# Forgetting attention and a bilinear feed-forward on one core: another source for the idle matmuls, masks on GpSimd for one more batch, merged reciprocals, and a new order on all engines

## The chip, the cores and the metric

The kernel runs on one core of a Trainium2 chip. The core has five engines that run their own instruction streams and wait for each other through semaphores: TensorE (PE, matrix products; its weight loads are shown as PEld), VectorE (DVE), ScalarE (ACT), GpSimd (POOL) and SyncE (SP, which here only issues transfers). Sixteen DMA engines move data between device memory and the on-chip buffer (SBUF), or within it; products land in PSUM. The metric is the time of one execution on the device in microseconds (us).

## What is computed

The attention scores of 8 batches with 8 heads, 576 positions and head size 64 get a decay from cumulated logarithms, a causal mask and a softmax; the result goes through a feed-forward part without a nonlinearity but for a product.

```python
scores = scale * np.matmul(q, k.transpose(0, 1, 3, 2))
log_f = np.log(np.clip(f, 0.0001, 1.0))
cum = np.cumsum(log_f, axis=-1)
decay = cum[:, :, :, None] - cum[:, :, None, :]
scores = np.where(causal, -1000000000.0, scores + decay)
attn = softmax(scores)            # along the last axis
x = np.matmul(attn, v)            # heads side by side: 4608 x 512
out = ((x @ w_a) * (x @ w_b)) @ w_out   # 512 -> 1536 -> 512
```

Inputs and outputs are float32; products take float16.

## The kernel before

A unit of attention is a head pair t = 4 b + pr: two heads of batch b, of 32 such pairs. The 576 queries are five blocks i = 0 to 4 (four of 128, one of 64). For each, PE forms the scores in PSUM (tile `sc`), DVE adds the decay and takes the row maximum (`do_decay`, L673, into `S`; in batch 0 the decay is added by PE and DVE only takes the maximum, `do_max`, L645), ACT takes the exponential and the row sums (`do_exp`, L704, into `PA` for blocks 0 to 2 and `PB` for blocks 3 and 4), DVE takes the reciprocal of the sums (`do_recip`, L712 and L714), POOL or ACT scales the rows with it (`do_norm`, L725 and L723), the scaled block is transposed (by PE into `psP` in batch 0 and for blocks 0 to 2 of batch 1, by DMA into `PTA` and `PTB` otherwise), and PE multiplies it with the values (`pv`, `pvx`). The rows of the decay for all keys stand in `spread`, three buffers that are used in turn; for batch 1 PE and an eviction fill them, later a DMA from `cum_d`.

The causal mask is made in two ways. For head pairs outside `MASKP` PE adds a product of two constants, `neg` and `low`, to the diagonal blocks of `sc`. For those in it, POOL writes masked copies of the diagonal blocks of `spread` (`mask_copy`, L630, and `mask_last`, L637), so that the decay carries the mask; PE then computes blocks 1 and 2 in two pieces, the diagonal block first. `PSPREAD` are the four pairs of batch 1, `EARLY` batches 0 and 1.

The feed-forward part runs over pieces of 256 to 512 tokens: PE forms `psa` and `psb` (L74), ACT copies `psa` to `a`, DVE multiplies (`ht`, L1072), PE forms `pso` and ACT or DVE evicts it (`osb`) for the store. The last 1024 tokens are done by a scheme with fewer products (tiles `wg`, `wb`, `og`, `om`), which fills the last 60 us. The feed-forward pieces of earlier batches fill PE between the attention steps of later ones.

At the start PE has nothing to do until q and k have landed. `wake` gives it idle matmuls, 24 times four, which read the identity matrix; their sums are never used. POOL issues the loads of the weights: each of w_a and w_b in four pieces, columns 0 to 511 and columns 512 to 1535, each for both halves of the partitions.

What sets the order: the kernel writes every step as an `Op` in a list and then runs through a table `ORDER` of their numbers. Each engine executes its own steps in that order, so a step that waits holds everything behind it on its engine. `CHOICE` says for each step that several engines could do which of them does it, and `SLOTS` which buffer of a ring each tile takes. SP's queue holds, in the order of that table as well, the loads of q, k and v, of `spread`, the transposing DMAs and the stores; POOL's queue holds the loads of the weights and of the first batches among its own work.

## Time and profile before

| | us |
|---|---|
| three runs | 392.8, 396.06, 396.86 |
| median | 396.06 |
| span of the profiled execution | 394.4 |
| busy in it: PE, DVE, ACT, POOL | 381.1, 329.1, 299.4, 281.0 |
| granted TensorE clock, mean | 0.999 |

The profiled execution's own time is given as its span, from the first to the last instruction; the time of a run has what lies around it as well. Busy times are unions of an engine's instructions. A matmul's end is modelled, and matmuls overlap, so the start of the next one tells what one costs. In the page's slices each digit is the busy share of a fortieth of the span in tenths:

```profile
DVE  7888898998996888788788888757898899987992
ACT  4998999999886878868888588779899672556331
POOL 8689686768867689874899769578976891267600
PEclk9999999999999999999999999999999999999999
```

The clock is granted in full throughout. DVE, ACT and POOL are all loaded in the first quarter, and POOL does nothing in the last slices.

### The profile page before, as it was taken

The numbers are of one execution on the slowest core, as the hardware profiler recorded it, in microseconds if no ns is written. First come the engines' busy times: TensorE is split into PE (matmuls) and PEld (weight loads), VectorE is DVE, ScalarE is ACT, GpSimd is POOL, SyncE is SP. The second block draws the span as 40 slices with busy tenths as digits, with TensorE's granted clock in tenths as the row PEclk, the third lists the DMA queues.
The fourth block names the chain that finished last, engine by engine and source line by source line (L and its number), as shares of the span: only waits on it lengthen the run. The fifth ranks groups of instructions, "written<-read, shape, count | busy, mean of one in ns | idle before, by whom it ended". The sixth has DMA issues, their size and how long they took to land.

```text
span 394.4 us, 14909 instructions
## 1 busy us (share of the span) xinstructions
PE 381.1 (97%) x5816; PEld 253.9 (64%) x5816; DVE 329.1 (83%) x1035; ACT 299.4 (76%) x826; POOL 281.0 (71%) x482
## 2 busy tenths in 40 slices
PE   7899999999998999999899999999999999999996
PEld 3557887968765665655555655555555667666796
DVE  7888898998996888788788888757898899987992
ACT  4998999999886878868888588779899672556331
POOL 8689686768867689874899769578976891267600
PEclk9999999999999999999999999999999999999999
DMA  7999999999999999999998999999998898100005
GB/s 121 251 202 170 144 154 223 228 278 275 208 222 215 220 282 247 281 187 277 260 237 255 262 207 229 206 244 263 226 226 195 169 182 178 55 1 2 2 2 214
DMA packets 147190, 76.88 MB, mean 195 GB/s; under 512 B 124336, under 2 KB 128176, under 8 KB 147120
## 3 DMA queue, kind: packets, MB, share of 16 engines
q1 hardware_dynamic: 132824, 68.79, 77.9%
q0 software_dynamic: 14256, 7.08, 14.7%
q8 instruction: 45, 0.74, 0.8%
q14 instruction: 25, 0.20, 0.2%
q10 hardware_dynamic: 40, 0.07, 0.1%
HBM read 52.05 MB, written 9.58 MB: 156 GB/s over the span
## 4 chain that ended last, share of the span: by engine, by line
PE 73%; DMA 11%; DVE 5%; POOL 4%; ACT 3%; issue 2%; ACTq 0%; DVEq 0%; POOLq 0%
PE psa L74 15%; PE psb L74 15%; PE pso L74 13%; PE wg L74 5%; DMA PTA<-PA 5%; PE wb L74 4%; PE sc L550 3%; PE og L74 3%; DMA PTB<-PB 3%; PE pvx L768 3%; PE psT L358 2%; DVE S L673 2%; DMA wb<-in_moe_w_b_dram 2%; POOL PA L725 2%; PE wake L74 2%
## 5 line engine op out<-in xcount | busy, mean ns | idle before, releaser
L673 DVE CUSTOM_DVE_ANT_0 S<-sc,spread 64x576 f32<-64x576 f32 (+4 forms) x232 | 125.5, 561 | 14.5 <-ACT PA L704 4.8
L725 POOL TENSOR_SCALAR PA<-PA,st 128x256 f16<-128x256 f16 (+2 forms) x180 | 85.0, 481 | 9.6 <-DVE st L714 6.0
L74 PE MATMUL psb<-xT,wb 128*64 128x512 f16 (+2 forms) x864 | 88.7, 332 | 0.4 <-DVE ht L1072 0.2
L704 ACT ACTIVATE PA<-S,st 128x256 f16<-128x256 f32 (+2 forms) x168 | 84.1, 503 | 6.4 <-DVE st L673 5.8
L74 PE MATMUL psa<-xT,wa 128*64 128x512 f16 (+2 forms) x864 | 88.9, 333 | 0.0
L74 PE MATMUL pso<-wout,ht 128*64 128x512 f16 x672 | 81.8, 381 | 0.0
L725 POOL TENSOR_SCALAR PB<-PB,st 128x512 f16<-128x512 f16 (+1 forms) x90 | 63.6, 713 | 25.3 <-DVE st L714 8.8
L74 PEld LDWEIGHTS <-wb 128*64 128x64 f16 x960 | 55.9, 110 | 24.9 <-issue 1.8
L74 PEld LDWEIGHTS <-wa 128*64 128x64 f16 x960 | 55.2, 110 | 24.7 <-issue 2.2
L1072 DVE TENSOR_TENSOR ht<-psb,a 128x512 f16<-128x512 f32 (+1 forms) x90 | 57.5, 648 | 7.2 <-PE psb L74 5.1
L288 ACT CAST a<-psa 128x512 f16<-128x512 f32 (+1 forms) x90 | 49.4, 550 | 18.0 <-PE psa L74 15.8
L74 PEld LDWEIGHTS <-ht 128*64 128x64 f16 x696 | 38.3, 110 | 26.8 <-issue 2.2
L704 ACT ACTIVATE PB<-S,st 128x512 f16<-128x512 f32 x56 | 40.2, 720 | 3.2 <-DVE st L673 2.7
L704 ACT ACTIVATION_READ_ACCUMULATOR PA<-S,st 128x1 f32 x168 | 32.1, 191 | 0.0
L630 POOL TENSOR_SCALAR_AFFINE_SELECT spread<-spread 128x768 f32<-128x768 f32 x24 | 20.8, 866 | 14.0 <-DMA spread<-cum_d 13.9
L700 ACT ACTIVATE PB<-S,st 128x576 f16<-128x576 f32 x28 | 21.7, 776 | 10.7 <-DMA PTB<-PB 4.1
L768 PEld LDWEIGHTS <-nv 128*64 128x64 f16 x640 | 21.8, 110 | 8.5 <-DMA PTA<-PA 2.3
L673 DVE CUSTOM_DVE_ANT_1 S<-sc,spread 128x256 f32<-128x256 f32 x48 | 19.7, 419 | 7.5 <-ACT PB L704 1.6
L1273 POOL TENSOR_TENSOR hy<-wu 128x512 f16<-128x512 f32 x9 | 11.6, 1302 | 19.7 <-DVE wu L1273 19.6
L714 DVE RECIPROCAL st<-st 128x2 f32<-128x2 f32 x128 | 18.1, 156 | 7.2 <-ACT PA L704 3.6
L673 DVE DVE_READ_ACCUMULATOR2_ANT st<- 128x1 f32 (+1 forms) x280 | 22.8, 81 | 0.0
L550 PE MATMUL sc<-kT,qT 64*128 64x512 f16 (+4 forms) x144 | 21.0, 326 | 1.2 <-ACT kT L288 0.4
(156 smaller groups left out, 692.8 us busy)
## 6 DMA issues: line engine op xcount, KB each, us to landing
spread<-cum_d SPq DMA_DIRECT2D x24, 576.0 KB, 6.4
q<-in_q_dram SPq DMA_DIRECT2D x14, 576.0 KB, 5.3
k<-in_k_dram SPq DMA_DIRECT2D x14, 576.0 KB, 5.4
out_dram<-osb SPq DMA_DIRECT2D x29, 256.0 KB, 4.0
v<-in_v_dram SPq DMA_DIRECT2D x24, 256.0 KB, 5.8
wout<-in_moe_w_out_dram POOLq DMA_DIRECT2D x3, 512.0 KB, 8.0
nv<-in_v_dram POOLq DMA_DIRECT2D x8, 128.0 KB, 5.1
wa<-in_moe_w_a_dram POOLq DMA_DIRECT2D x2, 512.0 KB, 7.5
```

The costliest lines, as they stand in the source:

```text
L74: nc.tensor.matmul(out=out[r], lhsT=lhsT[:, r], rhs=rhs, **kw)
L288: nc.scalar.copy(out=out_, in_=in_)
L550: nc.tensor.matmul(out=dst, lhsT=lhsT, rhs=rhs, start=start, stop=stop, skip_group_check=True)
L630: nc.gpsimd.affine_select(out=c[:, :, 0:SM].rearrange("p h (j k) -> p h j k", k=128), in_=c[:, :, SM:2 * SM].rearrange("p h (j k) -> p h j ...
L673: nc.vector.tensor_tensor_reduce(out=o, in0=x, in1=y, scale=-1.0, scalar=3e38, op0=ADD, op1=MIN, accum_out=m)
L700: nc.scalar.activation(out=p_blocks(t, 4), in_=T[("s" if direct else "z", t, 4)], func=EXP, bias=st[:, 8:9], scale=sign, accum_out=st[:, 1 ...
L704: nc.scalar.activation(out=p_blocks(t, i)[:, :, h, :], in_=(T[("s", t, i)][:, h, :] if direct else T[("z", t, i)][:, h * n:h * n + n]).rea ...
L714: nc.vector.reciprocal(out=st[:, 20 + 2 * i:22 + 2 * i], in_=st[:, 10 + 2 * i:12 + 2 * i])
L725: VEC[e].tensor_scalar(out=p, in0=p, scalar1=st[:, c:c + 1], scalar2=1.0, op0=MUL, op1=MUL)
L768: nc.tensor.matmul(out=o[HP[h], 128 * i:128 * i + 128], lhsT=vt[:, j, pr + NP * h, :], rhs=pt[:, base_blk[i] + 2 * block_at(t, i, j) + h, ...
L1072: nc.vector.tensor_tensor(out=ht[:, 0:n_], in0=T.pop(("psb", t0, fbs))[:, 0:n_], in1=T.pop(("a16", t0, fbs))[:, 0:n_], op=MUL)
L1273: VEC[e].tensor_tensor(out=out_, in0=x, in1=y, op=op)
```

## The change

Five things are changed.

1. The idle matmuls read a new tile `spark` (both as weights and as moving operand), which DVE sets to one in a step of its own.
2. `MASKP` takes in the four head pairs of batch 1. POOL writes masked copies for them; the last block of these pairs still gets its mask from PE.
3. Reciprocals are merged. For batches from 2 on one takes blocks 0 to 2 and one blocks 3 and 4; for batches 0 and 1 one takes blocks 0 and 1, one block 2, one blocks 3 and 4. A merged reciprocal needs all exponentials of its blocks, and every scaling of these blocks needs it.
4. Weight loads are issued in another order among POOL's steps.
5. `ORDER`, `CHOICE` and `SLOTS` are new tables. The number of steps falls from 2480 to 2401.

```diff
+    spark = perm.tile([128, 2], FP16, tag="spark", name="spark")
...
-            mm_halves(x, ident16, ident16[:, 0:1].to_broadcast([128, 512]), start=True, stop=True, skip_group_check=True)
+            mm_halves(x, spark[:, 0:1].to_broadcast([128, 128]), spark[:, 0:1].to_broadcast([128, 512]), start=True, stop=True, skip_group_check=True)
...
+    o_s = Op("DVE", 0.1, lambda _: nc.vector.memset(spark, 1.0), prio=-302, name="spark")
...
-        o = Op("PE", 0.427, lambda _: wake(2), [o_i], prio=-290, mode="full", name=f"wake{n}")
+        o = Op("PE", 0.427, lambda _: wake(2), [o_s], prio=-290, mode="full", name=f"wake{n}")
...
-    MASKP = {t for t in range(8, NP * B)}
+    MASKP = {t for t in range(4, NP * B)}
...
-        if g == 3 and t in MASKP:
+        if g == 3 and t in MASKP and t not in PSPREAD:
...
-    def do_recip(t, i):
+    RGROUPS = {True: [(0, 1, 2), (3, 4)], False: [(0, 1), (2,), (3, 4)]}
+
+    def do_recip(t, blocks):
         st = T[("st", t)]
-        if i == 4:
-            nc.vector.reciprocal(out=st[:, 28:29], in_=st[:, 18:19])
-        else:
-            nc.vector.reciprocal(out=st[:, 20 + 2 * i:22 + 2 * i], in_=st[:, 10 + 2 * i:12 + 2 * i])
+        c0, c1 = 2 * blocks[0], 9 if blocks[-1] == 4 else 2 * blocks[-1] + 2
+        nc.vector.reciprocal(out=st[:, 20 + c0:20 + c1], in_=st[:, 10 + c0:10 + c1])
...
-                rc = Op("DVE", 0.16, lambda _, i=i: do_recip(t, i), es, prio=prio(g))
-                st_users.extend(es + [rc])
...
+                for blocks in RGROUPS[b not in EARLY]:
+                    if i not in blocks or not all(x in ex_of for x in blocks):
+                        continue
+                    rc = Op("DVE", 0.16, lambda _, blocks=blocks: do_recip(t, blocks), sum((ex_of[x] for x in blocks), []),
+                            prio=prio(g), name=f"rc{t}.{blocks[0]}")
...
     ORDER = """
-        0 1 29 30 46 2 52 62 5 3 31 37 32 38 33-36 39 40 42 41 53 47 58 4 43 267 262 279 6-9 54 48 10 56 50 44
...
     CHOICE = """
-        DDDDADADADAAPPAPPPAPPAADAPPPPPPAPADDDDPPPAPPPPPDDDDPAAPAPPPADDDADAADAAAADDPPPAPAPPPADDAAPPAPPAPAADADAAA
...
+        DDPPAAADDDADPPPPPPPPPDDADAPPPPPAAPDDADAPPAPPPPPDDDAAAPAAPPPPADADDADDDDAADAPPAPPPPPPADDDPAPPPAPPPDAAAPA
```

What the tables do is seen on three engines. First ACT at the start of the program, before the change: after the two logarithms (`cum_l`) stand two evictions of the transposed q and k (`qT`, `kT`), the load of the table for the exponential, two more evictions, and the first exponentials (`PA`).

```order
L259 ACTIVATE cum_l<-cum_f 96x256
L259 ACTIVATE cum_l<-cum_f 96x320
L286 ACTIVATE qT<-psT 128x576
L288 COPY kT<-psT 128x576
L220 ACT_TABLE_LOAD
L220 ACTIVATE warm<-warm 128x1
L286 ACTIVATE qT<-psT 128x576 x2
L704 ACTIVATE PA,st<-sc_301,st 128x2x128
```

The same place on ACT after the change:

```order
L261 ACTIVATE cum_l<-cum_f 96x256
L261 ACTIVATE cum_l<-cum_f 96x320
L221 ACT_TABLE_LOAD
L221 ACTIVATE warm<-warm 128x1
L288 ACTIVATE qT<-psT 128x576
L290 COPY kT<-psT 128x576 x2
L706 ACTIVATE PA,st<-sc_257,st 128x2x128
```

The table load stands ahead of the first evictions now, and one eviction of k takes the place of two of q. On PE the transposes of the second half of q (from tile `wout`) stood ahead of the first scores and now stand behind them; and ahead of the very first transpose stand nine groups of four idle matmuls where five stood.

Second POOL, from the last setting of constants (`nv`) on, before the change; `PA<-PA` are scalings, `nv<-in_v_dram` loads of v, `wa` and `wb` loads of the weights, `q<-q` and `k<-k` conversions of the next batch:

```order
L113 MEMSET nv_80 64x512
L725 TENSOR_SCALAR PA<-PA,st 128x128
L620 MEMSET spread_84 128x2x64
L304 DMA nv_79<-in_v_dram 128x8x64 x2
L290 TENSOR_SCALAR q_470<-q_184 128x2x9x64
L725 TENSOR_SCALAR PA<-PA,st 128x2x128
L292 CAST k_473<-k_186 128x2x9x64
L725 TENSOR_SCALAR PA<-PA,st 128x2x128
L725 TENSOR_SCALAR PA<-PA,st 128x3x128
L509 DMA wa_76<-in_moe_w_a_dram 64x4x512
```

And after it:

```order
L114 MEMSET nv_81 64x512
L622 MEMSET spread_85 128x2x64
L511 DMA wa_77<-in_moe_w_a_dram 64x4x1024
L306 DMA nv_80<-in_v_dram 128x8x64 x2
L511 DMA wa_77<-in_moe_w_a_dram 64x4x512
L292 TENSOR_SCALAR q_520<-q_295 128x2x9x64
L511 DMA wb_78<-in_moe_w_b_dram 64x4x512
L727 TENSOR_SCALAR PA<-PA,st 128x2x128
L294 CAST k_535<-k_468 128x2x9x64
```

Three loads of weights stand ahead of the first scaling now, the first of them for columns 512 to 1535. The second piece of wa for columns 0 to 511 stood behind six scalings and stands behind thirteen; the last load of wb stood behind 21 scalings and four conversions and stands behind 17 and two. Two subtractions for the low parts of `crow`, which DVE did, stand on POOL ahead of the constants.

Third DVE in the middle of the program, before the change; `ISA S,st` are score additions with their maximum, `ISA st` reads of that maximum:

```order
L1072 TENSOR_TENSOR ht<-psb,a_4120 128x512
L673 ISA S,st<-sc_4047,spread_86 128x384
L673 ISA st 128x1
L1072 TENSOR_TENSOR ht<-psb,a_4173 128x512
L714 RECIPROCAL st<-st 128x2
L673 ISA S,st<-sc_4137,spread_86 64x576
L673 ISA st 64x1
L714 RECIPROCAL st<-st 128x2
L1072 TENSOR_TENSOR ht<-psb,a_4183 128x512
L712 RECIPROCAL st<-st 128x1
```

And after it:

```order
L675 ISA S,st<-sc_3979,spread_85 128x384
L675 ISA st 128x1
L1081 TENSOR_TENSOR ht<-psb,a_3972 128x512
L716 RECIPROCAL st<-st 128x6
L1081 TENSOR_TENSOR ht<-psb,a_4072 128x512
L716 RECIPROCAL st<-st 128x6
L675 ISA S,st<-sc_3974,spread_86 128x512
```

One reciprocal of six columns (blocks 0 to 2, two heads) takes the place of three of two columns, and one of three columns that of one of two and one of one.

On PE, in batch 1, the 64 products of `neg` and `low` for blocks 0 to 3 are gone, and 16 pieces of scores more are formed. Between the first scores of the last head pair and its output products stand 24 groups psa or psb and 10 groups pso (24 and 7 before); behind its scores of block 3 there stand 7 groups psa or psb and 8 pso (12 and 7 before).

More of the change, by code (lines that the diff above doesn't have):

```diff
@@ L154 @@
+        a0123456b78cd0192345678ab0123456789cd0;n16:01010100100100110110100010111101;n32:0120221021212012012002
+        102110202201201020120102012012012010012;nv:0101010101;osb:010111010010010101001010101101;qd:0101010101
+        00101010100101;sc:010101010101010101010101100101011001100001010101001010100110100101010101010100101010
+        1010100101010101010010001010010010100101010001010010101001010;st:01234501234501234501234051203401
     """
```

122 lines of the change are left out of this document (82 added, 40 removed), and 135 rows, old and new, of the table ORDER.

## The prediction

> **What bounds the kernel now.** I read the page first: its span, the busy shares and the slices of PE.
>
> ```profile
> span 394.4 us, 14909 instructions
> PE 381.1 (97%) x5816; PEld 253.9 (64%) x5816; DVE 329.1 (83%) x1035; ACT 299.4 (76%) x826; POOL 281.0 (71%) x482
> PE   7899999999998999999899999999999999999996
> ```
>
> TensorE (PE) is busy 97% of 394.4 us, so at most 394.4 - 381.1 = 13.3 us of open idle time are to be had. But "busy" includes the idle matmuls (tile wake), so I read the first 50 us by windows next. Columns: window, length, then busy us and instructions of PE, PEld, DVE, ACT, POOL.
>
> ```profile
> 10.00:20.00 10.00, 8.84 (x192) 5.28 (x186) 8.65 (x16) 9.70 (x38) 6.59 (x12) 1.00 1.14 253
> 20.00:30.00 10.00, 9.37 (x162) 5.82 (x160) 8.58 (x23) 9.23 (x30) 8.91 (x18) 1.00 1.00 199
> 30.00:40.00 10.00, 9.78 (x198) 7.38 (x196) 8.62 (x17) 8.99 (x22) 9.18 (x15) 1.00 1.08 172
> 40.00:50.00 10.00, 9.79 (x242) 8.67 (x238) 8.09 (x27) 9.23 (x26) 6.19 (x9) 1.00 1.21 134
> ```
>
> From 10 to 40 us ScalarE (ACT) has 27.9 of 30 us, VectorE (DVE) 25.9 and GpSimd (POOL) 24.7, the last of them 6.6 in the first ten and 9.2 in the last ten. This stage is bound by the chain of softmax work through all three, and PE waits for it with idle matmuls. From 40 us on PE is full, and there only work taken from PE, or a wait of PE, is worth anything. So there are two stages, with two kinds of price. The wait list of PE, of ACT in its last row (us in total, times, longest), shows what is left to win or lose in the second:
>
> ```profile
> PE pvx L768 <- DMA PTA<-PA: 2.0, 4, 0.7
> PE sc L538 <- DVE ht L1072: 1.1, 1, 1.1
> PE sc L74 <- DVE xT L292: 1.0, 1, 1.0
> ...
> ACT PB L700 <- DMA PTB<-PB: 4.1, 3, 2.9
> ```
>
> The first three are 4.1 us: all that PE stands still for long between 50 us and the end.
>
> **Part 1, the start.** These rows are the timeline of the first 12 us (start, duration, engine, line, operation, what ended the idle time).
>
> ```profile
> 0.88 0.06 DVE L215 MEMSET warm<- 128x1 f32 x1 [0.88 <-PEq L1710]
> 1.33 0.83 POOL L333 DMA_DIRECT2D k<-in_k_dram  x1 [0.81 <-POOLq L1710]
> 2.69 0.62 POOL L333 DMA_DIRECT2D q<-in_q_dram  x1
> 2.80 4.48 PE L74 MATMUL wake<-ident 128*64 128x512 f16 x20 [2.80 <-POOL ident masks.py:199]
> 7.21 0.69 PE L358 MATMUL psT<-ident,q 64*64 64x64 f16 x18
> 7.71 0.66 PE L358 MATMUL psT<-ident,k 64*64 64x64 f16 x18
> 8.30 1.06 PE L74 MATMUL wake<-ident 128*64 128x512 f16 x8
> 8.48 0.63 ACT L288 COPY kT<-psT 128x576 f16<-128x576 f16 x1
> 9.14 1.28 ACT L220 ACT_TABLE_LOAD   x1
> 9.29 0.48 PE L358 MATMUL psT<-ident,wout 64*64 64x64 f16 x36
> 9.70 0.34 PE L550 MATMUL sc<-kT,qT 64*128 64x256 f16 x4
> 11.60 0.48 ACT L704 ACTIVATE PA<-sc,st 128x256 f16<-128x256 f32 x1
> ```
>
> Idle matmuls: the constant is DVE's first instruction in the new order, so they can start near 0.88 + 0.06 = 0.94, call it 1.0, not 2.80. Nine groups of four now stand ahead of the first transpose, where five stood. The first 20 took 4.48 us, 224 ns each; the eight at 8.30 took 1.06, 133 ns each. If the slow pace again lasts 4.5 us, that is 20 of the 36, and 16 x 0.133 = 2.1 us follow: the block ends at 1.0 + 4.5 + 2.1 = 7.6. So it starts 1.8 us sooner and ends 0.3 us later than before. The change issues q first (at 1.33 in place of k) and k second (at 2.69, where q stood). q landed at 7.21 after its issue at 2.69, so k now lands near 7.2. With the idle block, the q transposes start at 7.6 and those of k end near 7.6 + 2 x 0.5 = 8.6, against 7.71 + 0.66 = 8.4: nothing is won by the idle matmuls themselves.
>
> The Trainium skill's page "TensorE: Matmul & The Clock Gate", section "Part 1: The HAM clock gate", says that the array runs at half speed until it has been busy for about 3.4 us. The trace is slower than that: 224 ns for all 20, up to 7.28. By the page 15 matmuls would be slow and the block would end near 1.0 + 3.4 + 21 x 0.133 = 7.2 (an estimate), and the sum below would be 0.4 us better.
>
> What is won stands on ACT and on PE's order. Before, the exp table was loaded between the evictions and the first exp, 9.14 to 10.4, and ACT then evicted two more q tiles until 11.60, while the scores began at 9.70, behind transposes that waited for the second q load until 9.29. Now the table load stands ahead of the first evictions, in time in which ACT waits for q and k, and the transposes of the second q stand behind the scores. k is evicted about 8.6 + 0.65 = 9.25, the scores start there (-0.45), and the first exp needs only them and the maximum: 11.60 - 9.70 = 1.9 us before, about 1.3 without the evictions in its way, so 10.6, 1.0 us earlier. From there to the first copy of the feed-forward part the order gives ACT one eviction less (0.63) and one scaling more (0.48): -0.15. ACT alone would give -1.2.
>
> POOL gives less. Its rows, and the two of PE that wait for it:
>
> ```profile
> 14.03 0.37 POOL L725 TENSOR_SCALAR PA<-PA,st 128x128 f16<-128x128 f16 x1 [2.84 <-DVE st L714]
> 14.51 1.82 POOL L304 DMA_DIRECT2D nv<-in_v_dram  x2
> 21.53 0.68 POOL L509 DMA_DIRECT2D wa<-in_moe_w_a_dram  x1
> 28.80 1.14 POOL L292 CAST k<-k 128x1152 f16<-128x1152 f32 x1
> ...
> 37.17 0.64 POOL L509 DMA_DIRECT2D wb<-in_moe_w_b_dram  x1
> ...
> 35.80 1.06 PE L74 MATMUL psa<-xT,wa 128*64 128x256 f16 x16
> 45.18 1.06 PE L74 MATMUL psb<-xT,wb 128*64 128x256 f16 x16 [0.21 <-DMA wb<-in_moe_w_b_dram]
> ```
>
> The first weight load moves from behind four scalings into POOL's idle 2.84 us. It is columns 512 to 1535 of half of wa; of the two pieces that the first psa needs, one moves up too, the other falls back from behind six scalings to behind thirteen. Ahead of the last wb issue stand 17 scalings instead of 21 (-4 x 0.48), 2 conversions instead of 4 (-2 x 1.14), one v load more (+0.91), one mask select more (+0.87), and two subtractions that were DVE's (about 0.5 each, +1.0): -1.4 us, more where idle time is filled. So wb lands earlier; but it held PE for only 0.21. The conversions and some scalings of the second head pair now come behind the weights, and PE needs them between the first psa and the third psb. Laying POOL's rows end to end in the new order I reach the first psa at about 34.5 (35.80 before) and the third psb at about 44.4 (45.18 before). Between -1.2 (ACT) and -0.8 (POOL) I take **-1.0**. Bounds: -3.3, if ACT's 30 - 27.9 = 2.1 us of idle time go as well, and +0.5, if POOL's three extra pieces (2.8 us) fall where it is full and its savings where it was idle.
>
> **Part 2, batch 1 masked by GpSimd.** PE's 64 mask matmuls of head pairs 4 to 7 go. Two rows of the timeline, then both kinds of select (count, busy, mean ns, idle before):
>
> ```profile
> 39.89 0.28 PE L550 MATMUL sc<-neg,low 64*128 64x64 f16 x8
> 40.01 0.43 PE L358 MATMUL psT<-ident,q 64*128 64x64 f16 x18
> ...
> L630 POOL TENSOR_SCALAR_AFFINE_SELECT spread<-spread 128x768 f32<-128x768 f32 x24 | 20.8, 866 | 14.0 <-DMA spread<-cum_d 13.9
> L637 POOL TENSOR_SCALAR_AFFINE_SELECT spread<-spread 128x256 f32<-128x256 f32 x24 | 9.7, 404 | 5.4 <-DVE st L673 5.3
> ```
>
> Eight masks delay the next matmul by 40.01 - 39.89 = 0.12 us, 15 ns each, though one lasts 190: they overlap. 64 x 15 ns = 0.96 us of PE. Blocks 1 and 2 are now computed in two pieces, 16 matmuls more with no column more: between 0 and 16 x 15 ns = 0.24 us. The same number of changes from one shape of matmul to another stays. I take **-0.8**, bounds -1.0 and -0.7. POOL pays 4 x (0.866 + 0.404) = 5.1 us between about 30 and 75 us. Cover: in 40 to 50 us it is idle 3.8 of 10. If that cover is gone, the score additions of DVE wait for the select; before, the selects waited 5.3 us for DVE.
>
> **Part 3, merged reciprocals.** From batch 2 on a head pair has two reciprocals instead of five, in batches 0 and 1 three: 24 x 3 + 8 x 2 = 88 fewer.
>
> ```profile
> 20.61 0.28 DVE L714 RECIPROCAL st<-st 128x2 f32<-128x2 f32 x3
> ...
> L714 DVE RECIPROCAL st<-st 128x2 f32<-128x2 f32 x128 | 18.1, 156 | 7.2 <-ACT PA L704 3.6
> ...
> L725 POOL TENSOR_SCALAR PA<-PA,st 128x256 f16<-128x256 f16 (+2 forms) x180 | 85.0, 481 | 9.6 <-DVE st L714 6.0
> L725 POOL TENSOR_SCALAR PB<-PB,st 128x512 f16<-128x512 f16 (+1 forms) x90 | 63.6, 713 | 25.3 <-DVE st L714 8.8
> ```
>
> Three in a row take 0.28, so about 0.08 each in the stream (0.156 alone): 88 x 0.08 = 7 us of DVE over 330 us, 2% of an engine that is not the bound. PE waited 1.1 + 1.0 us for DVE in all, so the gain is between 0 and -2.1. Against it: no scaling of blocks 0 to 2 can start before the last exp of block 2. Four scalings (4 x 0.48 = 1.9 us) that POOL could do in between now come behind it, ahead of the transposing DMA, for which PE waited 2.0 us in 4 waits. In PB the scaling of block 4 (0.71) moves behind the exps of block 3 likewise. Whether this reaches PE depends on the work in the order between scores and output products: for the last head pair 24 groups of psa/psb stand there as before, and 10 of pso instead of 7; but behind its scores of block 3 stand 7 groups of psa/psb instead of 12. I take **0**, between -2.1 and +7.6 (the 4 waits, each 1.9 longer).
>
> **Part 4, the rest of the new order.** Sums, loads and stores are the same in number; the slots of the rings are dealt anew. The 4.1 us of PE waits may shrink or grow; I take **0**, with -4.1 below (it includes the -2.1). In the last 60 us PE's slices are full before, and the same products stand there.
>
> **Sum.** -1.0 - 0.8 + 0 + 0 = -1.8 us: a span of 392.6. The runs took 392.8, 396.06 and 396.86; the page gives the profiled execution's span alone, 394.4, and that lies 1.7 under the median; what lies around the span is not shown. I set the difference on the median: 396.06 - 1.8 = 394.3.
>
> **Rivals.**
> 1. *The waits of the second stage go too.* For it: DVE is relieved of 7 us, and the PTA waits come from single late transposes. Against: the loads that crowd the queues are all still there. 394.3 - 4.1 = 390.2.
> 2. *The merged reciprocals make the transposes late.* Place: PE at the output products, waiting for PTA. For it: the 4 waits, and POOL's 6.0 us behind reciprocals. Against: 10 pso groups where 7 stood. Four tiles longer by 1.9: 394.3 + 7.6 = 401.9. One such tile takes the whole gain of 1.8.
> 3. *POOL eats the start.* Its load in 20 to 40 us is 18.1 of 20, and masks, subtractions and v load add 2.8. With the start at +0.5 and the masks' 0.8 paid back: 396.06 + 0.5 = 396.6, no change.
>
> **Chances.** A measurement of this kernel tells about 1%, 4 us, from no change. My forecast has 0.45, with its own range from 391.5 (start -3.3, DVE part of the waits) to 396.3; about a quarter of it lies below 392.1. Rival 1 has 0.27, nearly all of it faster; rival 2 has 0.16, nearly all slower; rival 3 has 0.12, spread over no change and somewhat slower. Faster 0.12 + 0.25 = 0.37; slower 0.15 + 0.03 = 0.18; within 1% the other 0.45. The range takes in rival 1 with the start at its best (390.2 - 2.3 = 387.9, cut to 388.5) and most of rival 2: 388.5 to 400.
>
> **What would show it.** Start: idle matmuls from 1.0 us, first exp near 10.6, first psa near 34.5, third psb near 44.4; if the third psb is at 45 or later, step 1 is wrong. Masks: 64 products sc<-neg,low with 64*128 where 128 were, eight more POOL selects, and no new wait of DVE for spread. Reciprocals: 72 rows, and PE's wait for PTA at 2.0 us or less; 5 or more would be rival 2. Waits of PE after 50 us near 4; near 1 would be rival 1. The prediction is wrong if third psb comes early and the end does not, or if PE waits for PTA more than twice as long as before.

## The result and the profile after

| | before | after |
|---|---|---|
| runs of the comparison, us | 392.8, 394.41, 396.06, 396.86 | 398.97, 399.6, 401.14, 401.21 |
| median | 395.24 | 400.37 |
| span of the profiled execution | 394.4 | 397.3 |
| its first `psa`, third `psb`, us from the start | 35.80, 45.18 | 39.72, 49.03 |

The kernel became slower, by 1 to 2%: the ratio is 1.0153, with a 95% interval of 1.011 to 1.0197 (the two medians alone give 1.013). The forecast was 394.3 us. Here and below a ratio leaves out the executions in the slow state (one of a1's 12, three of e2's 6, one of e3's 8, some of the kernel before's), while the medians are of all.

First the page of the profile after; the digits are the slices of the span, as before.

```profile
span 397.3 us, 14723 instructions
PE 382.7 (96%) x5768; PEld 252.8 (64%) x5768; DVE 324.0 (82%) x950; ACT 296.9 (75%) x820; POOL 290.7 (73%) x494
...
PE   8799999989999999999899999999999999999996
...
PEclk9899999999999999999999999999999999999999
```

PE has 48 matmuls less and DVE 5.1 us less to do, as the change intends. What stands out is the second slice, at about 10 to 20 us: PE is less busy there, and the granted clock is not full. The windows of the same kernel show it closer (window, length, busy us and instructions of PE, PEld, DVE, ACT, POOL, then granted clock, DMA share, GB/s):

```profile
14.80:17.00 2.20, 1.95 (x56) 1.25 (x56) 0.00 (x0) 1.63 (x6) 2.12 (x3) 0.74 1.06 367
17.00:19.30 2.30, 2.24 (x16) 0.68 (x12) 1.76 (x4) 1.66 (x9) 1.15 (x2) 0.51 1.22 208
10.00:20.00 10.00, 7.41 (x144) 3.75 (x142) 6.06 (x13) 7.01 (x30) 7.74 (x17) 0.83 1.14 277
```

From 10 to 20 us ACT is busy 7.0 us where it was 9.7, DVE 6.1 where it was 8.65. So PE, ACT and DVE waited for something there; POOL is busier than before (7.7 us, 6.6 before). The timeline of after (start, duration, engine, line, operation, idle time before and its releaser) names it:

```profile
1.00 5.19 PE L75 MATMUL wake<-spark 128*64 128x512 f16 x24 [1.00 <-DVE warm L216]
...
6.76 1.40 POOL L103 TENSOR_SCALAR_AFFINE_SELECT low<-low 64x128 f16<-64x128 f16 x2
8.11 0.73 POOL L335 DMA_DIRECT2D wout<-in_q_dram  x1
8.38 0.34 PE L552 MATMUL sc<-kT,qT 64*128 64x256 f16 x4 [0.18 <-ACT kT L290]
10.10 0.47 ACT L706 ACTIVATE PA<-sc,st 128x256 f16<-128x256 f32 x1
14.84 0.48 PE L360 MATMUL psT<-ident,wout 64*64 64x64 f16 x36 [2.19 <-DMA wout<-in_q_dram]
15.37 0.65 ACT L288 ACTIVATE qT<-psT 128x576 f16<-128x576 f16 x1 [2.11 <-PE psT L360]
17.04 2.19 PE L75 MATMUL wake<-spark 128*64 128x512 f16 x8
20.95 0.47 POOL L727 TENSOR_SCALAR PA<-PA,st 128x256 f16<-128x256 f16 x1 [2.79 <-DVE st L716]
39.72 1.06 PE L75 MATMUL psa<-xT,wa 128*64 128x256 f16 x16
49.03 1.06 PE L75 MATMUL psb<-xT,wb 128*64 128x256 f16 x16 [0.48 <-ACT a L290]
```

Up to 10 us the change wins: the first scores start at 8.38 (9.70 before) and the first exponential at 10.10 (11.60 before). Then the second half of q, loaded into the tile `wout`, is issued by POOL at 8.11, behind the selects that set the constants. Its transposes on PE wait 2.19 us for it, ACT and DVE behind them, and the first feed-forward product comes 3.9 us later than before. In the kernel before, the timeline has that load ahead of the constants:

```profile
3.32 0.72 POOL L333 DMA_DIRECT2D wout<-in_q_dram  x1
```

The chain of work that ended last in after goes through that load too (start, length, what):

```profile
6.81 1.30 POOL low L103 x2
8.11 6.69 DMA wout<-in_q_dram
...
14.84 0.51 PE psT L360 x35
```

The load took 6.69 us from issue to landing, and what set its issue was POOL's work on constants. It landed at 14.80, where it had landed at 8.85 in the kernel before.

From the third `psb` to the end the profiled execution of after takes 397.3 - 49.03 = 348.3 us, that of before 394.4 - 45.18 = 349.2. So this pair of executions puts the whole loss into the first 50 us. The medians differ by 5.1 us and the two profiled executions by 2.9; they lie on the near sides of their medians (398.97 against 400.37, 396.06 against 395.24), which makes the other 2.2 us.

### The profile page after: what moved, and what is told of

Read it like the earlier page. It is cut to its first block, busy times and chain, and to the rows that moved or that the text cites. A ratio compares the mean times of both kernels' runs of the same rounds, so it can differ in the third digit from the quotient of the medians.

```text
span 397.3 us, 14723 instructions
## 1 busy us (share of the span) xinstructions
PE 382.7 (96%) x5768; PEld 252.8 (64%) x5768; DVE 324.0 (82%) x950; ACT 296.9 (75%) x820; POOL 290.7 (73%) x494
## 4 chain that ended last, share of the span: by engine, by line
PE 71%; DVE 8%; DMA 7%; POOL 5%; issue 4%; ACT 4%; SPq 0%; POOLq 0%; DVEq 0%; ACTq 0%
PE pso L75 13%; PE psa L75 13%; PE psb L75 13%; PE wg L75 5%; PE wb L75 4%; PE sc L552 4%; DVE S L675 3%; PE pvx L770 3%; PE og L75 3%; DMA PTB<-PB 3%; PE wake L75 2%; PE psP L75 2%; PE psT L360 2%; PE sc L540 2%; DMA wout<-in_q_dram 2%
## 5 line engine op out<-in xcount | busy, mean ns | idle before, releaser
L675 DVE CUSTOM_DVE_ANT_0 S<-sc,spread 64x576 f32<-64x576 f32 (+3 forms) x224 | 121.5, 568 | 19.7 <-PE sc L75 5.4
L727 POOL TENSOR_SCALAR PA<-PA,st 128x128 f16<-128x128 f16 (+2 forms) x179 | 84.5, 484 | 25.8 <-DVE st L716 15.3
L75 PE MATMUL pso<-wout,ht 128*64 128x512 f16 x672 | 80.2, 380 | 0.1
L727 POOL TENSOR_SCALAR PB<-PB,st 128x512 f16<-128x512 f16 (+1 forms) x93 | 66.4, 723 | 12.8 <-DVE st L716 9.3
L632 POOL TENSOR_SCALAR_AFFINE_SELECT spread<-spread 128x768 f32<-128x768 f32 x28 | 24.2, 868 | 3.9 <-DMA spread<-cum_d 3.7
L675 DVE CUSTOM_DVE_ANT_1 S<-sc,spread 128x256 f32<-128x256 f32 x56 | 22.8, 418 | 4.9 <-ACT PB L702 2.2
L552 PE MATMUL sc<-kT,qT 64*128 64x512 f16 (+5 forms) x160 | 20.5, 313 | 0.6 <-ACT qT L288 0.2
L647 DVE TENSOR_REDUCE st<-sc 128x2 f32<-128x512 f32 (+4 forms) x20 | 15.5, 802 | 5.7 <-PE sc L552 5.7
```

Source lines behind the costliest of these rows:

```text
L75: nc.tensor.matmul(out=out[r], lhsT=lhsT[:, r], rhs=rhs, **kw)
L552: nc.tensor.matmul(out=dst, lhsT=lhsT, rhs=rhs, start=start, stop=stop, skip_group_check=True)
L632: nc.gpsimd.affine_select(out=c[:, :, 0:SM].rearrange("p h (j k) -> p h j k", k=128), in_=c[:, :, SM:2 * SM].rearrange("p h (j k) -> p h j ...
L647: nc.vector.tensor_reduce(out=m, in_=T[("s", t, i)], axis=AXX, op=MAX, negate=True)
L675: nc.vector.tensor_tensor_reduce(out=o, in0=x, in1=y, scale=-1.0, scalar=3e38, op0=ADD, op1=MIN, accum_out=m)
L727: VEC[e].tensor_scalar(out=p, in0=p, scalar1=st[:, c:c + 1], scalar2=1.0, op0=MUL, op1=MUL)
```

## The experiments

Each ratio is to runs of the kernel before beside it on the same chip. The last columns are of one profiled execution each (a dash where none is given), and they vary between executions: a7 and a9 differ by one move far behind the start, a8 and a10 by the same one, and their first `psa` stand 1.7 and 0.7 us apart.

| run | starts from | median us, before's beside it | ratio, 95% interval | first `psa`, third `psb` us |
|---|---|---|---|---|
| a1 | after | 396.61, 393.92 | 1.0052, 1.0018 to 1.0087 | 37.50, 46.82 |
| b1 | before | 400.53, 393.92 | 1.0139, 1.0087 to 1.0191 | 42.09, 52.82 |
| a2 | after | 399.5, 393.92 | 1.0135, 1.0078 to 1.0193 | 39.52, 48.91 |
| a5 | after | 399.98, 393.92 | 1.0147, 1.0085 to 1.0209 | 39.15, 48.46 |
| a4 | after | 398.45, 393.12 | 1.0124, 1.008 to 1.0167 | 37.01, 46.32 |
| m1 | after | 401.27, 393.12 | 1.0193, 1.0142 to 1.0245 | 39.03, 48.35 |
| a6 | a1 | 396.85, 393.12 | 1.0082, 1.0051 to 1.0114 | 39.45, 48.76 |
| a7 | a6 | 395.17, 393.12 | 1.0056, 1.0025 to 1.0087 | 35.01, 44.32 |
| b3 | before | 395.11, 393.13 | 1.0041, 1.0007 to 1.0075 | 36.04, 45.33 |
| a8 | a7 | 395.07, 393.13 | 1.005, 1.0014 to 1.0086 | 34.78, 44.10 |
| a9 | a7 | 396.41, 393.13 | 1.0083, 1.0057 to 1.011 | 36.71, 46.02 |
| a10 | a8 | 396.51, 393.13 | 1.0086, 1.0049 to 1.0124 | 34.11, 43.42 |
| d1 | a8 | 390.82, 393.37 | 0.9933, 0.9907 to 0.9959 | 35.36, 44.67 |
| d2 | before | 395.8, 393.37 | 1.0077, 1.0047 to 1.0106 | 36.04, 49.29 |
| e1 | a8 | 407.1, 394.17 | 1.0307, 1.0254 to 1.036 | 34.39, 43.70 |
| e2 | a1 | 413.1, 394.17 | 1.0391, 1.0317 to 1.0464 | - |
| e3 | a8 | 397.88, 393.52 | 1.0109, 1.0066 to 1.0151 | - |

No kernel that does the whole work beats the kernel before (d1 and d2 leave 16 stores out). The edits are moves in the table `ORDER`; they are shown as rows of the engine's stream.

### One load: a1 and b1

Theory 1 is that the place of the second q load on POOL's queue makes the loss. Theory 2 is that the merged reciprocals do, since POOL's first scaling waits 2.79 us for one. a1 puts the load back ahead of the constants; b1 makes the same fault in the kernel before, where the load goes from ahead of them to behind them. POOL's stream in a1:

```diff
 L335 DMA wout_79<-in_k_dram 128x2x576
+L335 DMA wout_79<-in_q_dram 128x2x576
 L98 AFFINE_SELECT neg_60<-neg_60 64x64
 L103 AFFINE_SELECT low_61<-low_61 64x128
...
 L103 AFFINE_SELECT low_62<-low_62 64x128
-L335 DMA wout_79<-in_q_dram 128x2x576
 L233 TENSOR_TENSOR crow<-cum_f,crow 32x320 x2
```

> The changed kernel with one move on GpSimd's queue: the load of q's second columns (the one into wout) is issued right behind k's second load, ahead of the constants' selects, so at about 5.2 us where the changed kernel issued it at 8.11. Theory 1 (the late load): it lands at about 12 (the load took 6.7 us from issue to landing), TensorE's wait of 2.19 us ahead of the second group of transposes out of wout at 14.84 falls under 0.5, the granted clock, 0.74 and 0.51 between 14.8 and 19.3 us in the changed kernel, stays at 1.00, the first psa comes at 36 to 37 us in place of 39.72, and the time is 3 to 4 us below the changed kernel's 400.4, at 396 to 397.5. Theory 2 (the merged reciprocals and the scalings behind them set the start): the wait goes, but the first psa stays within 1 us of 39.7 and the time within 1 us of 400.4. Theory 3 (the new order as a whole, the loss spread over 10 to 40 us): first psa 38 to 39, time 398.5 to 399.5.

> The kernel before with one move on GpSimd's queue: the load of q's second columns, issued at 3.32 us, goes behind the constants' selects, so that it is issued at about 7.7 and lands at about 13.5 to 14.5. Theory 1: the first transposes out of wout, at 9.29 in the kernel before, wait until then, a gap of 4 to 5 us with a clock near 0.5 for some microseconds behind it; first psa 40 to 42 in place of 35.80 and time 399 to 402 against 395.2: one load's place is enough to lose what the change lost. Theory 2 or 3 (the load's place costs little, since other work follows it): time within 1.5 us of 395.2.

a1 takes the ratio from 1.0153 to 1.0052, and b1 brings the kernel before to 1.0139. About two thirds of the loss hang on one row of one queue, and a1's interval does not meet that of after. a1's timeline of PE has the wait at 0.51:

```profile
13.35 0.48 PE L360 MATMUL psT<-ident,wout 64*64 64x64 f16 x36 [0.51 <-DMA wout<-in_q_dram]
```

and b1's has it at 5.14, since there PE meets those transposes earlier in its order:

```profile
14.14 0.70 PE L358 MATMUL psT<-ident,wout 64*64 64x64 f16 x36 [5.14 <-DMA wout<-in_q_dram]
```

Theory 1 holds. But a1's first `psa` stands at 37.5, still 1.7 later than before, and 0.5% of the time is left. a1 does not give the load its old place either: it is issued at 5.23 there, behind five loads of q and k and not behind two, takes 8.08 us and lands at 13.31. PE waits 0.51 for it, so not much more can hang on it directly; no run issues it sooner in the new order.

### The slow clock behind the wait: a2

Behind the 2.19 us of idle PE the granted clock is 0.74 and then 0.51, and eight idle matmuls take 2.19 us. The page "TensorE: Matmul & The Clock Gate" of the Trainium skill, section "Part 1: The HAM clock gate", lists two states, full and half rate, and gives an idle window of about 3.4 us ahead of the fall. The half rate agrees with 0.51; the fall came after less idle time than that. Whether it costs anything was a part of Theory 1, called 1a. a2 leaves the load late and moves three groups of four idle matmuls from behind the wait into it:

```diff
 L552 MATMUL sc_389<-neg_60,low_62 128x64
+L75 MATMUL wake<-spark 64x512
...
 L360 MATMUL psT<-ident_70,wout_79 64x64
```

> The changed kernel with the load left late (issued at 8.11, landing at 14.8), but three groups of idle matmuls that stood behind the second transposes out of wout put ahead of them, so that TensorE is busy for most of the 2.19 us in which it waited. Theory 1a (the wait costs twice, itself and a lower clock behind it): the granted clock between 14.8 and 19.3 us is 1.00 in place of 0.74 and 0.51, which gives back some 1.1 us on eight idle matmuls (2.19 us against 1.06) and 0.4 us on the scores; the three groups have left the way behind the wait too, 1.5 us more: first psa 2 to 3.3 us earlier than 39.72, time 397 to 398.5. Theory 1b (only the wait counts, the clock does not hang on it): the clock stays low in that stretch, first psa about 1.5 us earlier, time near 399. Theory 2 (scalings): first psa within 1 us of 39.7, time within 1 us of 400.4.

The clock stayed at 1.00, as a window of a2 shows, and the time stayed too:

```profile
17.00:19.30 2.30, 1.54 (x16) 0.79 (x16) 2.30 (x7) 2.08 (x12) 0.93 (x3) 1.00 1.22 196
```

a2's timeline of PE shows new gaps instead, for the work that had come late with q:

```profile
17.43 0.34 PE L552 MATMUL sc<-kT,qT 64*128 64x384 f16 x2 [0.99 <-ACT PA L706]
...
26.80 0.53 PE L75 MATMUL psP<-ident,PA 128*64 128x128 f16 x12 [1.32 <-POOL PA L727]
```

Theory 1a falls as far as these runs resolve (an interval of 0.5% each way). The slow matmuls of after were eight idle ones and, ahead of them, the scores of one block, which took 0.96 us up to the idle ones (0.55 in a1). At the full clock the next scores start at 17.43 in a2, not at 19.16, but behind ACT and POOL that gain is lost: the first `psa` comes 0.2 us sooner. One of the four executions of after had a mean clock of 1.000, and took 399.6.

### Reciprocals and masks by themselves: a5, a4, m1

a5 moves the first merged reciprocal of each of the four head pairs of batch 0 forward on DVE. a4 computes one reciprocal for each block again, where the merged one stands. m1 gives the masks of batch 1 back to PE: its functions for the masks test the set `MASKF` in place of `MASKP`. The diff is a4's, with m1's line at its end.

```diff
-        c0, c1 = 2 * blocks[0], 9 if blocks[-1] == 4 else 2 * blocks[-1] + 2
-        nc.vector.reciprocal(out=st[:, 20 + c0:20 + c1], in_=st[:, 10 + c0:10 + c1])
+        for x in blocks:
+            c0, c1 = 2 * x, 9 if x == 4 else 2 * x + 2
+            nc.vector.reciprocal(out=st[:, 20 + c0:20 + c1], in_=st[:, 10 + c0:10 + c1])
...
+    MASKF = {t for t in range(8, NP * B)}
```

> The changed kernel with the four merged reciprocals of blocks 0 and 1 of the first batch (tiles 0 to 3) put earlier in VectorE's queue, each right behind the last maximum that its exponentials' end allows; the merging stays and the late load stays. Theory 1 (the late load): GpSimd's wait of 2.79 us ahead of its first scaling at 20.95 falls by 2 us or more, but TensorE's wait of 2.19 us and the low clock stay, the first psa stays within 0.7 us of 39.72 and the time within 1 us of 400.4. Theory 2 (scalings behind merged reciprocals set the start): first psa 1.5 us or more earlier and time at 398.5 or below.

> The changed kernel with every merged reciprocal issued as separate ones again, at the same place in VectorE's queue: 88 more instructions of VectorE, nothing moved. Were the merging worth what a row says of one reciprocal in a run (0.28 us for three, 0.22 for two, so 0.07 to 0.09 more each), VectorE is busy 6 to 8 us longer of 324. If merging is a step of no weight (the term 0 of the forecast), the time is within 1.5 us of 400.4 and the first psa within 0.7 us of 39.72. If VectorE holds others up, the time rises by 3 us or more.

> The changed kernel with the masks of batch 1 back on TensorE, every other instruction at its place: 64 mask matmuls more, 16 of the split score matmuls fewer, and GpSimd's eight selects of batch 1 gone (5.1 us). By the forecast's term for this step (0.8 us on TensorE's path) the time rises by 0.8, to 401.2, which the interval can hardly tell from 400.4; TensorE's instructions are busy about 0.7 to 0.9 us longer. If GpSimd's selects delay the scalings of the start, the first psa comes 0.5 to 1 us earlier than 39.72 and the time falls by as much.

In a5 POOL's first scaling starts at 18.16 without a wait, 2.8 us sooner, and nothing is won: the conversion of k behind it then waits 1.03 us for its load, and PE waits for q as before. Theory 2 falls as the first cause. a4 has DVE busy 328.9 us (324.0 merged) at a ratio that cannot be told from after's. It prices the instructions alone, since each scaling still waits for all reciprocals of its group. m1 has 48 matmuls more and POOL at 286.4 us, and its interval overlaps after's likewise. So neither part weighs anything that these runs resolve. a4's profile is of use in another way: the load of q was issued at 8.07 there as well, but took 5.34 us, PE waited 0.85, the clock stayed at 1.00, and the first `psa` came at 37.01.

### What stands behind the load: a6, a7, b3, a8

With q on time, three more things could hold the start. a6 is a1 with a5's reciprocals and with six scalings of the first two head pairs, where one stood, ahead of the conversion of k on POOL. a7 also leaves out 6 of the 24 groups of idle matmuls, those that stood in runs of two or three. b3 leaves six groups out of the kernel before. a8 is a7 with the first piece of wa behind v on POOL, and batch 1's k ahead of batch 2's q on SP.

```diff
-        o = Op("PE", 0.427, lambda _: wake(2), [o_s], prio=-290, mode="full", name=f"wake{n}")
+        o = Op("PE", 0.427, lambda _, n=n: wake(0 if n in {3, 4, 9, 10, 15, 19} else 2), [o_s], prio=-290, mode="full", name=f"wake{n}")
```

```diff
 L624 MEMSET spread_85 128x2x64
-L513 DMA wa_77<-in_moe_w_a_dram 64x4x1024
 L308 DMA nv_80<-in_v_dram 128x8x64 x2
...
 L513 DMA wb_78<-in_moe_w_b_dram 64x4x512
+L513 DMA wa_77<-in_moe_w_a_dram 64x4x1024
 L729 TENSOR_SCALAR PA<-PA,st 128x2x128 x2
```

> The early load of the first experiment, and besides it the four merged reciprocals of tiles 0 to 3 put sooner (as in the third experiment) and, on GpSimd's queue, the four scalings of tile 0 and both of tile 1's block 1 put ahead of the cast of the next k, which waits for its load. Theory A (two waits stand side by side: behind the late load, GpSimd's scalings are the next to be late): TensorE's wait of 0.53 us for a scaling ahead of its first probability transposes at 24.77 goes, first psa 36.5 to 37.2 in place of 37.50, time 395 to 396.5 against 396.6 for the early load alone. Theory B (what is left of the loss is the idle matmuls' place on TensorE, which runs them whether it need or not): first psa within 0.6 us of 37.5.

> The kernel of the run before it with 6 of the 24 groups of idle matmuls left out, all of them from runs of two or three groups between 20 and 35 us (24 of 96 idle matmuls; their results are read by nobody). A run of groups into one buffer takes 0.68 us a group, so 4.1 us of TensorE are taken out. Theory B (idle matmuls on the path): first psa 33.5 to 35, time 2 to 4 us under the kernel with them. Theory A (the scalings, exponentials and their maxima set the pace, the idle matmuls fill what would be waits): TensorE's gaps grow by nearly what was taken out, first psa within 1 us of that kernel, time within 1 us. A clock below 1.00 between 20 and 40 us would add time under both.

> The kernel before with six of its 24 groups of idle matmuls left out, from between 17 and 34 us, everything else as it was. In that kernel GpSimd's scalings and weight loads are the chain from 21 to 36 us and few groups follow one another in one buffer. Theory B' (idle matmuls fill waits there): first psa within 0.8 us of 35.80, time within 1 us of the kernel before. If idle matmuls lie on the path there too, first psa 33.5 to 34.8 and time 1 to 2 us less. If TensorE then idles enough for the clock to fall, the time rises.

> The kernel with the early load, the sooner scalings and six groups of idle matmuls less, and in it two loads put back behind what is needed sooner: the first piece of wa behind the loads of v on GpSimd's queue, and q of batch 2 behind k of batch 1 on SyncE's. Theory C (the weights issued ahead hold up v and k): v, issued at 13.5 and landing at about 25.6 to 27 in that kernel and the one before it, lands before 22 us; TensorE waits for no v (0.2 us in the kernel it is made from, 1.6 us in the one before, where the clock then fell to 0.55); the cast of the next k waits for no load; the time is 0 to 1.5 us under 395.2 and its scatter smaller. If the transfers share the same sixteen engines anyway and only change places, the first third of wa comes late instead and the first psa waits: first psa at 36 or later, time 396 or above.

a6 lost its profiled start to the next late load, as the timeline of its PE shows: v, which POOL issues behind the first piece of wa.

```profile
26.35 0.30 PE L770 MATMUL pv<-xT,nv 128*64 128x128 f16 x4 [1.25 <-DMA nv<-in_v_dram]
26.98 0.25 PE L770 MATMUL pv<-xT,nv 128*64 128x128 f16 x2 [0.33 <-DMA nv<-in_v_dram]
```

In a7 idle matmuls take 13.0 us up to the first `psa` (summed from the start of each to that of the next instruction, less PE's idle time where it is over 0.1 us), against 17.7 in after and 14.7 before, and the first `psa` comes at 35.01, 0.8 us ahead of the kernel before. In b3 gaps took the place of the idle matmuls and nothing was won, so in the old order they only filled time. Its interval even lies above 1; whether leaving them out has a price in a7 and a8 too was not tested. a8 removes the waits for v and k as well and starts at 34.78. Yet a7 and a8 stand at 1.0056 and 1.005, where a1 stood with its first `psa` 2.5 us later. In these executions the start was won, and the time was given back later.

### Given back from 100 to 235 us: a9, a10, d1, d2

Where it was given back can be read by counting PE's 864 matmuls of `psa` in each profiled execution:

| | before | after | a1 | a7 | a8 | a9 | a10 | d1 | d2 |
|---|---|---|---|---|---|---|---|---|---|
| the 346th starts at, us | 123.2 | 125.5 | 122.3 | 119.7 | 120.3 | 121.0 | 119.0 | 120.0 | 128.1 |
| from it to the 605th, us | 109.7 | 110.6 | 109.3 | 113.9 | 113.5 | 113.1 | 112.6 | 107.9 | 107.9 |

a8 is 2.9 us ahead of the kernel before at the 346th and 0.9 behind it at the 605th; from there to the end both take some 161.5. The wait list for 100 to 235 us shows what came in. First the row of before, then that of after:

```profile
ACT PB L700 <- DMA PTB<-PB: 3.2, 2, 2.9
```

```profile
ACT PB L702 <- DMA PTB<-PB: 3.0, 2, 2.3
```

then the same list of a8, with the waits of PE that come of it:

```profile
PE psa L75 <- DVE st L677: 2.1, 1, 2.1
PE pvx L772 <- DMA PTA<-PA: 1.4, 2, 1.1
...
ACT PB L704 <- DMA PTB<-PB: 7.6, 4, 2.6
```

An exponential into the buffer `PB` must wait until the DMA that transposes its last contents into `PTB` is through. In before and after that takes 3.2 and 3.0 us in two waits, in a8, which comes there about 5 us sooner than after, 7.6 in four (in a1 2.0 in two). The longest goes on through DVE to PE. PE's own waits in this stretch are 3.2 us in before, 1.8 in after and 4.4 in a8. Theory D was that one transposing DMA stands too late on SP's queue, behind loads; a9 is a7 with that DMA moved ahead of two loads of k, and a10 is the same with a8's moves. Theory F was that the transfers as a whole set this stage: d1 is a8 without the stores of the first 2048 rows of the output (16 stores of 256 KB), d2 the kernel before without them.

```diff
 L1129 DMA out_dram<-osb 128x512
-L342 DMA k_4713<-in_k_dram 128x2x576
+L743 DMA_TRANSPOSE PTB<-PB_83 128x13x128
 L342 DMA k_4715<-in_k_dram 128x2x576
 L1129 DMA out_dram<-osb 128x512
-L743 DMA_TRANSPOSE PTB<-PB_83 128x13x128
 L743 DMA_TRANSPOSE PTA<-PA 128x12x128
+L342 DMA k_4845<-in_k_dram 128x2x576
```

```diff
+        if r0 < 2048:
+            return
         nc.sync.dma_start(out=out[r0:r0 + 128, :], in_=T.pop(("osb", t0, tb)))
```

> The kernel with the early load, the sooner scalings and six groups of idle matmuls less, and in it one move on SyncE's queue far behind the start: the transposes of tile 16's PB are issued ahead of the load of batch 5's first k, and the load of batch 6's first k behind tile 16's other transposes. Theory D (these transposes are late): ScalarE waits 2.3 to 2.6 us for them at about 188 us of the changed kernel, VectorE and then TensorE wait for ScalarE (1.8 and 2.1 us), and a wait of over 2 us lowers the clock behind it; with the move the wait falls under 0.8 us and the time by 1.5 to 3 us, to 392.5 to 394. If the transposes' source is what is late (the scaling of tile 16 ends at about 178), or if the load of k is then late, the wait moves to the next instruction and the time stays within 1 us of 395.2.

> Both of the moves of the two runs before together. Theory C and D: 1.5 to 4 us under 395.2, so 391.5 to 394 and the first variant of this study at or under the kernel before (393.1 in the last comparison). If either theory is wrong, the time is that of the better of the two alone.

> The kernel with the early load, the sooner scalings, six groups of idle matmuls less and the two loads put back, and in it the stores of the output's first 2048 rows left out: 16 of 256 KB, some 9 of every 100 bytes that move before 190 us, and 16 entries of SyncE's queue. Theory F (from 170 to 210 us the transfers and SyncE's queue set the pace, so that an earlier start is given back there): TensorE's waits of over 0.3 us between 100 and 235 us, 5.4 us together in that kernel's profile, shrink to under 2.5 us, the low clock at 189 us goes, and the time is 2.5 us or more under 395.1, at 392.6 or less. Theory G (the waits there come from the order in which the engines hand work to one another, not from the transfers): the waits stay within 1 us of what they were, the time within 1 us of 395.1.

> The kernel before with the same 16 stores left out. Theory F: the kernel before, whose transfers are as dense, gains too, 1 us or more (its waits of over 0.3 us between 100 and 235 us are 4.8 us together). If only the changed order is held up by its transfers, the kernel before gains under 0.5 us. Theory G: within 0.5 us of the kernel before, as the other run stays within 1 us.

a9's transposing DMA landed 6.0 us after its issue in place of 11.1, and the waits moved on. Its list for the same stretch has the price of the two loads that stepped back:

```profile
POOL k L296 <- DMA k<-in_k_dram: 8.2, 2, 5.5
ACT PB L704 <- DMA PTB<-PB: 4.7, 3, 2.5
```

So Theory D falls as a cure: the one wait went, and loads that are needed as soon came late. Without the stores, d1 took 4.25 us less than a8 (390.82 against 395.07), and its list is all but empty of waits for transfers:

```profile
PE pvx L772 <- DMA PTA<-PA: 0.2, 1, 0.2
ACT PB L704 <- DMA PTB<-PB: 0.2, 1, 0.2
```

Theory F holds in this form: the orders differ in this stage by what the stores cost them. Without the stores both take 107.9 us in the table above (one execution each), so what a8 takes more than the kernel before goes with the stores. That a7 to a10 lose there because they come sooner is argued: a1, at most 3.3 us behind them, takes 109.3. d2 missed its expectation and became slower. With the first store gone from SP's queue the loads of later batches are issued at 30.20 and 34.04 us, beside the weights that the start needs, and d2's PE waits for those:

```profile
43.69 1.06 PE L74 MATMUL psa<-xT,wa 128*64 128x256 f16 x16 [1.19 <-DMA wa<-in_moe_w_a_dram]
...
49.29 1.55 PE L74 MATMUL psb<-xT,wb 128*64 128x256 f16 x16 [2.51 <-DMA wb<-in_moe_w_b_dram]
```

Its third `psb` comes 4.1 us later than before's for that. From there to the end it takes 396.0 - 49.29 = 346.7 us, 2.5 less than the kernel before, so the stores cost the old order time behind the start too. At the start they had helped it: the first store, waiting on the queue, had kept these loads back. In d2 the larger pieces of `wa` (columns 512 to 1535) take 10.0 us to land and those of `wb` 11.9, in the kernel before 7.5 each.

### Bytes or the queue: e1, e2, e3

The stores could cost their bytes, or their places on SP's queue, where each waits for its copy while transposes stand behind. e1 is a8 with the same 16 stores issued on ScalarE's queue, at the same places of the table; e2 is a1 with that edit; e3 is e1 with each store right behind its copy.

```diff
-        nc.sync.dma_start(out=out[r0:r0 + 128, :], in_=T.pop(("osb", t0, tb)))
+        (nc.scalar if r0 < 2048 else nc.sync).dma_start(out=out[r0:r0 + 128, :], in_=T.pop(("osb", t0, tb)))
```

> The kernel with the early load, the sooner scalings, six groups of idle matmuls less and the two loads put back, and in it the 16 stores of the output's first 2048 rows issued from ScalarE's queue in place of SyncE's; every byte still moves. Leaving them out took 4.2 us off (395.07 to 390.82) and all but 0.4 us of TensorE's waits of over 0.3 us between 100 and 235 us. Theory F1 (what held the stage was the place in SyncE's queue that each store takes ahead of transposes and loads): most of that comes without leaving anything out, the time is 391 to 392.5, under the kernel before. Theory F2 (it was the 4 MB themselves, on sixteen engines that are busy in every slice): the waits come back, the time is 394.5 to 396. Should ScalarE wait at the stores for their copies, its exponentials come later and the time rises over 396.

> The changed kernel with the early load alone (396.6) and the same 16 stores issued from ScalarE's queue. Theory F1: 2 us or more under 396.6, at 392.5 to 394.5, the difference to the run beside it being what the fewer idle matmuls and the order of the start are worth once the later stage doesn't take it back (1 to 3 us). Theory F2: within 1 us of 396.6.

> The repaired kernel with the same 16 stores on ScalarE's queue, but now each right behind the copy that it stores (or four of ScalarE's steps behind it where VectorE made the copy). Where they stood before, up to 76 of ScalarE's steps behind the copy, the two output buffers came free late: copies waited for them 8.4 us on VectorE and 3.2 us on ScalarE, and the time was 407.1. Theory F1 (the place in SyncE's queue held the stage): 390.5 to 393. Theory F2 (the bytes did): 394 to 396.5, about the 395.1 of the same kernel with the stores on SyncE's queue. Over 398 would say that an issue on ScalarE costs more than the 0.34 us that the profile shows for it.

e1 and e2 measured another thing: at their places of the table the stores stand up to 76 steps of ACT behind their copies, so the output buffers come free late. The wait list of e1:

```profile
DVE osb L296 <- DMA out_dram<-osb: 8.4, 2, 6.1
PE psb L75 <- DVE osb L296: 4.5, 1, 4.5
```

e3 mends most of the loss and gets 1.0109, no better than a8 (1.005). The page "DMA: Bandwidth & Descriptors" of the Trainium skill, section "Rules for kernel authors", says that spreading transfers over the issuing engines brings no bandwidth, since all use the same DMA engines; e3 agrees. It does not settle the question: in its profiled execution DVE still waited 7.0 us for output buffers, and that execution took 402.75 us, 4.9 over the median. Whether the stores cost by their bytes, by the buffers that they hold or by their place in SP's queue stays open.

## Why the prediction was wrong

**Part 1, the start (-1.0, bounds -3.3 and +0.5): wrong by 4.9 us, and the failed step.** At the first `psa` it measured +3.9. What failed is that the later place of the second q's transposes was booked as a gain, while their load had moved back too. The first half came out. The idle matmuls start at 1.00, and the first exponential came at 10.10, 0.5 us sooner than forecast. One count was wrong, there as in the description of the change: six groups of idle matmuls stand ahead of the first transpose, not nine, so the block ended at 6.2 and not at 7.6, to PE's good. Then the prediction said that "the transposes of the second q stand behind the scores" and booked this as pure gain. It did not ask why they had been put there. Their load had moved on POOL's queue as well, from 3.32 to 8.11 us, behind the selects of the constants. The prediction listed POOL's order from the first weight load on, counted scalings and conversions, and of the loads ahead of it followed "q first (at 1.33 in place of k) and k second", but not the later pieces. a1 and b1 show that this one row is worth about 1.0 to 1.4% of the time. The first `psa` was forecast at 34.5 and came at 39.72. Its own sign of a wrong first step, a third `psb` at 45 or later, came true: 49.03. That the measured 400.4 lies next to the end of the stated range, 400, is luck: that end was set for rival 2. Nor does the forecast's own range, 391.5 to 396.3, come out of its terms: with the start at its best and DVE's waits gone it is 394.3 - 2.3 - 2.1 = 389.9, with start and masks at their worst 394.3 + 1.5 + 0.1 = 395.9.

**Part 2, masks (-0.8).** The count is right: 64 masks less and 16 pieces more make 48 matmuls less on the page. The size is not shown. The profiled executions take 349.2 - 348.3 = 0.9 us less from the third `psb` on, but other things changed there as well, and undoing the masks alone (m1) cannot be told from nothing. The selects went from 24 to 28 of each kind, as forecast, and DVE has no new wait for `spread`: 2.4 us in all, 3.4 before.

**Part 3, merged reciprocals (0, bounds -2.1 and +7.6).** Right as far as the runs resolve. DVE fell by 5.1 us (7 forecast). Taking the merging apart (a4) gives it 4.9 back and costs no time that can be told. The longer wait of the scalings was undone in no run; a5 shortened it in batch 0 and won nothing. Rival 2 gave 401.9, near the result, but for another reason: it had PE waiting for `PTA` at the output products, and in after's wait list these rows are gone.

**Part 4 (0, with -4.1 below).** The waits of PE went and came, as the wait list of after shows:

```profile
PE psT L360 <- DMA wout<-in_q_dram: 2.2, 1, 2.2
PE psa L75 <- DVE st L675: 1.8, 1, 1.8
PE psP L75 <- issue: 1.1, 1, 1.1
...
PE psb L75 <- DVE ht L1081: 0.6, 1, 0.6
```

Behind 50 us it holds 1.8 + 1.1 + 0.6 = 3.5 us of such waits, where 4.1 stood. The 1.8 is new, and the timeline of after shows that it comes from a transposing DMA, through ACT and DVE to PE:

```profile
191.69 0.77 ACT L702 ACTIVATE PB<-S,st 128x576 f16<-128x576 f32 x1 [2.29 <-DMA PTB<-PB]
192.59 0.42 DVE L675 CUSTOM_DVE_ANT_1 S<-sc,spread 128x256 f32<-128x256 f32 x1 [2.00 <-ACT PB L702]
193.07 1.05 PE L75 MATMUL psa<-xT,wa 128*64 128x512 f16 x8 [1.80 <-DVE st L675]
```

The forecast of "near 4" was right for after itself. What it did not see is what transfers and stores cost this stage: a good start was not worth its full size either (a7 to a10).

**Rival 3** had the right place, POOL's queue at the start, with a chance of 0.12 and too small a price: it counted three added pieces of work (+0.5), and not a load that they would stand ahead of.

What stays open is the last 0.5% between a8 and the kernel before: the stage from the 346th to the 605th `psa` accounts for its size in the profiled executions, but which moves of the new order cause the waits there was not isolated, nor whether they are of bytes, buffers or the queue.

## What to carry to other kernels

Where an order changes, follow every load on the queue that issues it, from the program's first row on, and write beside each consumer that moved back where its load went: a consumer that comes later is often the trace of a load that comes later. An engine that issues loads among its own work delays them by that work (here by 4.8 us), so loads that the critical chain needs first go ahead of constants that it needs last. And a gain at the start is worth what the next bound stage lets through: look there for waits on transfers before it is booked.

## What the runs showed of the hardware

The granted clock fell to half already after pauses of PE of little more than 2 us. In after it was 0.51 behind a wait of 2.19 us, in b1 0.50 behind 5.14. In the middle of a7 one wait of 2.08 was enough; its timeline and its windows:

```profile
188.05 1.05 PE L75 MATMUL psa<-xT,wa 128*64 128x512 f16 x8 [2.08 <-DVE st L677]
...
190.19 1.97 PE L75 MATMUL psa<-xT,wa 128*64 128x512 f16 x8
```

```profile
188.00:189.30 1.30, 1.25 (x12) 0.84 (x13) 1.30 (x8) 1.30 (x7) 0.83 (x2) 1.00 0.95 288
189.30:192.60 3.30, 3.30 (x19) 1.90 (x16) 1.95 (x7) 1.83 (x6) 2.20 (x4) 0.51 1.17 279
```

The clock is still full for 1.3 us after the wait, then half for 3.3, so the slow products are not the ones right behind it: eight matmuls of `psa` take 1.97 us in place of 1.05. The fall in after has the same shape: PE starts again at 14.84, the clock is 0.98 until 15.90 and 0.50 from there to 19.20.

The length of one pause does not settle it. In after itself a wait of 1.80 us at 191 to 193 us was followed by a full clock, while in a6 two shorter ones, the 1.25 and 0.33 us for v, were followed by this:

```profile
29.40:32.20 2.80, 2.70 (x32) 1.86 (x32) 1.50 (x5) 0.00 (x0) 2.80 (x5) 0.55 1.02 149
```

A page that shows a low clock in one slice is therefore read together with the waits a few microseconds earlier, and with what ran in it: in after that was one block's scores and idle matmuls, and a full clock there (a2) did not show in the time.
